# Two buffers for the halves of a slice, and another order of loads, in a fused attention and gMLP block

## The chip, the cores and the metric

The kernel runs on one core of one Trainium2 chip. The metric is the device time of one execution in microseconds (us); three timed runs of the kernel before gave 698.01, 703.25 and 704.19 us, so the median is 703.25 us.

## The reference

The input is one sequence of S = 2048 rows of D = 1024 bf16 numbers. First comes a pre-normalised attention with a sliding, dilated window (8 keys, every second row back), then a pre-normalised gated MLP that mixes the rows with a 2048 x 2048 matrix `w_sp`:

```
h  = x + attention(layernorm(x), wqkv) @ wo
z  = gelu(layernorm(h) @ w_in)            # [S, 3584], halves z1 and z2 of 1792 columns
z2 = layernorm(z2)
g  = einsum('ts,bsf->btf', w_sp, z2) + b_sp
out = h + (z1 * g) @ w_out                # w_out: [1792, 1024]
```

## The kernel before, in words

The first part, up to about 429 us of the profiled execution, computes the attention and both halves of z. Its instructions are ordered by a small planner in the kernel itself. z1 (transposed) and z2 are written to memory on the device, `z1_d` and `z2_d`, and read back later. The change does not touch this part, except that the first w_out load is issued near its end.

The second part is written out by hand, instruction by instruction, and so is the order of the DMA queue of SyncE (SP) in it. It runs two passes (`pr` = 0 and 1), each over 1024 rows t of the result. A pass has NQ = 7 groups (`i` = 0 to 6); group n = 7 pr + i takes 256 columns of z2 and forms w_sp @ z2 for them by Strassen's scheme: seven products instead of eight. Each product is eight matmuls of 128x128 by 128x512 (`times`, L1091). In a group the TensorE order is fixed: k1 (straight from the slice, block a11), k4, k3, k2 (from differences and sums of blocks of the slice, the tiles `zs`, made by `z_form` on VectorE one group ahead), then the second halves of k1 (block a12), k4 (block a22) and k3 (`zs` number 4). A slice is 2048 rows by 256 columns, 1 MB, held as [128, 16, 256]: its first half (row tiles 0 to 7) holds a11 and a21, its second half (row tiles 8 to 15) a12 and a22. `load_z2f(n, hf)` loads half hf of slice n; `z_form(n+1, 3)` reads the first half of slice n+1 alone, `z_form(n+1, 1)` both halves.

While a group's products run, ScalarE copies the first parts of k1, k4 and k3 out of PSUM (L1228 to L1232, into `p`), then does two side jobs of the first pass: row sums of |w_sp| (`row_sum`, L908, of rows that ScalarE itself loads as `wn`, L904) and column sums of |w_out| (`wout_sum`, L1135). VectorE makes the four `zs` of the next group (L988) and then the results of this one: L1285, L1290, L1292, the scaling of z1 (`z1_scaled`, L1145 on ScalarE or L1147 on VectorE), L1298 to L1300. GpSimd (POOL) adds in L1244, L1286, L1287 and L1291.

In group 5 of the first pass the scales are derived: `row_scales(1)` (L912 to L918) needs all row sums, `wout_level` (L1151 to L1156) all w_out sums, and both follow, in VectorE's order, everything that VectorE does for group 4. Two small transposes on TensorE (L1238, L1239) take their results. They stand in TensorE's order between k2 and the second part of k1 of group 5.

Four kinds of loads feed the first pass:
- z2 slices, one per group, two groups ahead, on SP's queue (L980);
- z1 pieces, `z1c`, 512 KB per group, one group ahead, on SP's queue (L1104); it waits for VectorE's L1300 of the group before, which frees its buffer;
- the next pass's part of w_sp, transposed on the way in by DMA (`load_raw(2, ...)`, L953, tile `rawa`), in four quarters of 512 KB, on SP's queue, in groups 1 to 4;
- w_out, 3.5 MB, on GpSimd's queue (`load_wout`, L1140), in groups 0 to 4.

The order on SP's queue in a group is: z1 piece n+1, at the group's end both halves of slice n+2, then the transposed quarter.

Of the kernel before, what the change touches and what calls it, by code (L numbers as in the profile page):

```python
# [11 lines left out]
BF16 = mybir.dt.bfloat16  # L12
# [10 lines left out]
P = 128  # L23
NT = S // P
CH = 512
NCH = S // CH
TPC = CH // P
# [19 lines left out]
HK = S // P // 2  # L47
# [85 lines left out]
def kernel(  # L133
# [14 lines left out]
    dma = nc.sync.dma_start  # L148
    dma_w = nc.gpsimd.dma_start
# [38 lines left out]
    def wtile(shape, name, tag):  # L188
        return w16.tile(shape, BF16, name=name, tag=tag)
# [760 lines left out]
    def load_raw(c, lo=0, hi=TPC):  # L950
        if lo == 0:
            raw[c] = wtile([P, NT, CH], "rawa", "wB") if c % 2 == 0 else zpools["z"].tile([P, NT, CH], BF16, name="rawb")
        nc.sync.dma_start_transpose(raw[c][:, :, lo * P:hi * P], wsp_view[c * CH + lo * P:c * CH + hi * P])  # L953
# [19 lines left out]
    z2f, zs = {}, {}  # L973
    z2_view = z2_d[:].rearrange("(k p) f -> p k f", p=P)

    def load_z2f(n, hf):
        if hf == 0:
            z2f[n] = zpools["z"].tile([P, NT, 2 * P], BF16, name="z2f", tag="z2f", bufs=2)
        i = n % (NF // 2)
        dma(z2f[n][:, hf * HK:(hf + 1) * HK, :], z2_view[:, hf * HK:(hf + 1) * HK, 2 * i * P:(2 * i + 2) * P])  # L980

    def z_form(n, m):
        z = z2f[n]
        a11, a21, a12, a22 = z[:, 0:HK, 0:P], z[:, 0:HK, P:2 * P], z[:, HK:NT, 0:P], z[:, HK:NT, P:2 * P]
        t = zs[n, m] = zpools["z"].tile([P, HK, P], FP16, name="zs", tag="zs", bufs=5)
        x, y, op = {3: (a11, a21, ALU.subtract), 1: (a21, a22, ALU.add), 2: (zs[n, 1][:] if m == 2 else None, a11, ALU.subtract),
                    4: (a12, zs[n, 2][:] if m == 4 else None, ALU.subtract)}[m]
        V.tensor_tensor(t[:], x, y, op=op)  # L988
# [37 lines left out]
    zpools = {}  # L1026
# [60 lines left out]
    NQ = NF // 2  # L1087

    def times(dst, wts, mov, first, lo=0, hi=HK, last=HK):
        for k in range(lo, hi):  # L1090
            T.matmul(dst, wts(k), mov(k), start=(first and k == 0), stop=(k == last - 1), skip_group_check=not first)  # L1091

    def slab(t):
        return lambda k: t[:, k, :]

    def f32(name):
        return p2.tile([P, CH], FP32, name=name, tag=name)
# [3 lines left out]
    def load_z1c(n):  # L1101
        pr, i = divmod(n, NQ)
        z1cs[n] = p2.tile([P, 2, 2 * CH], BF16, name="z1c", tag="z1c", bufs=2)
        dma(z1cs[n][:], z1_d[2 * i:2 * i + 2, :, 2 * pr * CH:(2 * pr + 2) * CH].rearrange("f p s -> p f s"))  # L1104
# [2 lines left out]
        hrs[t] = p2.tile([P, D], BF16, name="hr", tag="hr", bufs=4)  # L1107
        dma(hrs[t][:], h_d[t * P:(t + 1) * P, :])

    WLOAD = ((0, 4), (4, 8), (8, 10), (10, 12), (12, 14))  # L1110
    WSUM = {1: (0, 1, 2, 3), 2: (4, 5, 6, 7), 3: (8, 9, 10), 4: (11, 12, 13)}
    Z1ACT = (0, 5, 6) + tuple(range(NQ, 2 * NQ))

    small = p2.tile([P, 64], FP32, name="small", tag="small", bufs=1)
# [20 lines left out]
        A.activation(zg[:, NF - 1, :], wout_tile(f), ACTF.Abs, accum_out=l1n[:, f:f + 1])  # L1135

    def load_wout(i):
        lo, hi = WLOAD[i]
        dst = wout_a[:, lo:hi, :] if hi <= 8 else wout_b[:, lo - 8:hi - 8, :]
        dma_w(dst, wout_view[:, lo:hi, :])  # L1140

    def z1_scaled(n):
        z1c, s_ = z1cs[n], sf[:, n % NQ:n % NQ + 1]
# [62 lines left out]
    for pr in range(NCH // 2):  # L1206
# [4 lines left out]
        bt2 = bB[:, (2 * pr + 1) * CH:(2 * pr + 2) * CH]  # L1211
        for i in range(NQ):
            n = pr * NQ + i
            z = z2f[n]
            a11, a12, a22 = z[:, 0:HK, 0:P], z[:, HK:NT, 0:P], z[:, HK:NT, P:2 * P]
            p1, p7, p5, u = f32("p1"), f32("p7"), f32("p5"), f32("u2")
            if n == 0:
                load_z1c(0)
            if n + 1 < 2 * NQ:
                load_z1c(n + 1)  # L1220
            if i == 0:
                zg = p2.tile([P, NF, 2 * CH], FP16, name="zg", tag="zg", bufs=1)
            if n < len(WLOAD):
                load_wout(n)
            z1c = z1cs[n][:].bitcast(FP16)
            k1, k4, k3, k2 = bank_a(), bank(), bank(), bank()
            times(k1[:], slab(a11), slab(b11), True)
            A.copy(p1[:], k1[:])  # L1228
            times(k4[:], slab(zs[n, 3]), slab(t3), True)
            A.copy(p7[:], k4[:])  # L1230
            times(k3[:], slab(zs[n, 1]), slab(t1_), True)
            A.copy(p5[:], k3[:])  # L1232
            times(k2[:], slab(zs[n, 2]), slab(t2_), True)
            if pr == 0 and i == 5:
                row_scales(1)
                wout_level()
                turned = bank(BF16)
                T.transpose(turned[0:TPP, 0:P], rsc16[:, TPP:NT], ident[:])  # L1238
                T.transpose(turned[0:1, P:2 * P], kb[:, 0:1], ident[:])  # L1239
                A.copy(rscT[0:TPP, :], turned[0:TPP, 0:P])  # L1240
                A.dma_start(rs_d[TPP:NT, :], rscT[0:TPP, :])
            times(k1[:], slab(a12), slab(b21), False)
            times(k4[:], slab(a22), slab(t4_), False)
            nc.gpsimd.tensor_tensor(p7[:], p7[:], p5[:], op=ALU.add)  # L1244
            if pr == 0:
                if 1 <= i <= 4:
                    for t in (TPP + 2 * i - 2, TPP + 2 * i - 1):
                        row_sum(t, 0)
                        row_sum(t, 1)
                if i <= 3:  # L1250
                    load_wn2(TPP + 2 * i)
                for f in WSUM.get(i, ()):
                    wout_sum(f)
                if i == 6:
                    for fp in range(1, 5):
                        wout_scaled(fp)
            if i + 1 < NQ:
                for m in (3, 1, 2, 4):
                    z_form(n + 1, m)
                if n == 0:  # L1260
                    V.memset(ones[:], 1.0)
                    feature_scales()
            elif pr == 1:
                for m in (3, 1, 2, 4):
                    s_form(TPC, m, 0, NQ - 1)
            else:
                for fp in range(5, NQ):
                    wout_scaled(fp)
                scale_raw(2, 0)
                scale_raw(2, HK)  # L1270
            if pr == 0 and i == 5:
                wout_turned(turned[0:1, P:2 * P])
                spread = bank()
                T.matmul(spread[:, 0:2], ones[:], kb[0:1, 2:4], start=True, stop=True)
            times(k3[:], slab(zs[n, 4]), slab(b22), False)
            if n + 2 < 2 * NQ:
                for hf in range(2):
                    load_z2f(n + 2, hf)
            if pr == 0 and 1 <= i <= TPC:
                load_raw(2, i - 1, i)  # L1280
            elif n == 5:
                rows_in(1)
            if n in Z1ACT:
                z1_scaled(n)
            V.tensor_tensor(u[:], k2[:], p1[:], op=ALU.add)  # L1285
            nc.gpsimd.tensor_tensor(p1[:], u[:], bt1, op=ALU.add)  # L1286
            nc.gpsimd.tensor_tensor(u[:], u[:], bt2, op=ALU.add)  # L1287
            z11, z12 = zg[:, 2 * i, 0:CH], zg[:, 2 * i, CH:2 * CH]
            z21, z22 = zg[:, 2 * i + 1, 0:CH], zg[:, 2 * i + 1, CH:2 * CH]
            V.tensor_tensor(z11, k1[:], bt1, op=ALU.add)  # L1290
            nc.gpsimd.tensor_tensor(z22, p7[:], u[:], op=ALU.add)  # L1291
            V.tensor_tensor(z21, k4[:], p1[:], op=ALU.add)  # L1292
            if pr == 0 and i == 5:
                wout_spread(spread)
                wout_scaled(0)
            if n not in Z1ACT:
                z1_scaled(n)
            V.tensor_tensor(zg[:, 2 * i + 1, :], zg[:, 2 * i + 1, :], z1c[:, 1, :], op=ALU.mult)  # L1298
# [8 lines left out]
        for q in range(TPC):  # L1307
# [34 lines left out]
            a11, a12, a22 = slab(zz[:, 0, :, c1:c1 + P]), slab(zz[:, 1, :, c1:c1 + P]), slab(zz[:, 1, :, c2:c2 + P])  # L1342
# [94 lines left out]
```

## Time and profile before

| | us |
|---|---|
| median of three timed runs | 703.25 |
| the profiled execution, its own time | 708.02 |
| its span, first to last instruction | 706.2 |
| TensorE busy in the span | 686.5 (97%) |
| VectorE busy | 556.8 (79%) |
| ScalarE busy | 342.4 (48%) |
| GpSimd busy | 159.4 (23%) |
| group 0 of the first pass starts | 429.2 |
| group 6 of the first pass starts | 513.0 |

The profile is of one execution; the time outside its span is 708.02 - 706.2 = 1.8 us. "Idle before" an instruction is how long its engine stood still ahead of it, and the arrow names what ended this. SPq, ACTq and POOLq are the engines' own instruction streams where they issue DMAs; the time of such an issue ends when the engine has handed over its last descriptor, not when the data has landed.

### The profile page before, as it was taken

The page shows a single profiled execution, that of the slowest core. Times are in us where ns is not written, and L with a number is a line of the kernel's source. Part 1 is how long each engine was busy: PE and PEld are TensorE (multiplying, and loading weights), DVE is VectorE, ACT ScalarE, POOL GpSimd, SP SyncE. Part 2 cuts the span into 40 slices and gives each one's busy share as a digit, 9 for nine tenths or more (in the row PEclk, how much of TensorE's full clock was granted, in tenths as well). Part 3 has the DMA queues.
Part 4 walks back from the last instruction along what each step waited for, and adds up shares of the span by engine and source line. Part 5 has one row for each costly group of instructions (what it writes and reads, how often), then busy time and mean ns, then how long its engine had stood idle before and what let it go on. Part 6 is the DMA issues. An engine that isn't in the chain of part 4 may idle for free.

```text
span 706.2 us, 8977 instructions
## 1 busy us (share of the span) xinstructions
PE 686.5 (97%) x3374; PEld 354.5 (50%) x3374; DVE 556.8 (79%) x693; ACT 342.4 (48%) x493; POOL 159.4 (23%) x142
## 2 busy tenths in 40 slices
PE   9999999999999999999999999998699999999996
PEld 7766665566645445444444544443244434444443
DVE  6899899999999799997974485662879778665574
ACT  4547652444328876747754643685370322323231
POOL 0100010011010111100301212443340544543443
PEclk9999999999999999999999999999899999999999
DMA  9978597587994588461946996899676115553032
GB/s 322 321 232 246 161 222 244 150 235 216 269 357 124 164 229 231 168 161 34 204 172 172 243 302 210 270 234 232 156 203 184 59 61 151 149 146 92 0 120 89
DMA packets 145275, 133.05 MB, mean 188 GB/s; under 512 B 68752, under 2 KB 117296, under 8 KB 145104
## 3 DMA queue, kind: packets, MB, share of 16 engines
q1 hardware_dynamic: 132720, 88.93, 45.0%
q0 software_dynamic: 7856, 32.97, 17.0%
q10 hardware_dynamic: 4656, 10.59, 4.4%
q8 instruction: 26, 0.43, 0.3%
q14 instruction: 17, 0.14, 0.1%
HBM read 75.25 MB, written 33.10 MB: 153 GB/s over the span
## 4 chain that ended last, share of the span: by engine, by line
PE 77%; issue 8%; DMA 5%; POOL 5%; DVE 4%; SPq 0%; DVEq 0%; ACT 0%; POOLq 0%
PE acc L464 22%; PE acc L796 14%; PE acc L864 14%; PE bank L1091 12%; PE acc L719 8%; PE banka L1091 5%; DMA z2f<-z_d 2%; PE acc L306 2%; DMA hr<-h_d 2%; POOL p L1383 1%; POOL p L1382 1%; DMA rows<-rs_d 1%; DVE hr L1388 1%; PE wps L228 1%; POOL p L1363 1%
## 5 line engine op out<-in xcount | busy, mean ns | idle before, releaser
L864 PE MATMUL acc<-hnT,win 128*128 128x512 bf16 x448 | 98.0, 379 | 0.0
L796 PE MATMUL acc<-win,hnT 128*128 128x512 bf16 (+1 forms) x512 | 98.0, 352 | 0.0
L528 DVE TENSOR_TENSOR prod<-qT,kT 128x4096 bf16<-128x4096 bf16 x32 | 72.7, 2283 | 1.3 <-ACT kT L470 1.3
L796 PEld LDWEIGHTS <-hnT 128*128 128x128 bf16 x512 | 49.9, 98 | 47.4 <-issue 0.7
L1091 PEld LDWEIGHTS <-zs 128*128 128x128 f16 x448 | 43.6, 98 | 54.5 <-DVE zs L988 2.6
L864 PEld LDWEIGHTS <-win 128*128 128x128 bf16 x448 | 43.6, 98 | 52.6 <-issue 0.7
L475 ACT CAST stg<-acc 128x1024 bf16<-128x1024 f32 x36 | 36.4, 1012 | 61.1 <-PE acc L464 52.6
L1091 PE MATMUL banka<-rawa,z2f 128*128 128x512 f16 x224 | 54.2, 386 | 3.2 <-ACT p L1228 2.2
L464 PE MATMUL acc<-xnT,wk 128*128 128x512 bf16 x256 | 56.5, 379 | 0.0
L464 PE MATMUL acc<-xnT,wv 128*128 128x512 bf16 x256 | 56.4, 380 | 0.0
L719 PE MATMUL acc<-wo_sb,av_oT 128*128 128x512 bf16 x256 | 56.1, 379 | 0.0
L1091 PEld LDWEIGHTS <-z2f 128*128 128x128 bf16 x336 | 33.0, 99 | 44.3 <-issue 4.6
L1091 PE MATMUL bank<-rawb,zs 128*128 128x512 f16 x224 | 53.0, 379 | 1.3 <-DVE zs L988 1.3
L1091 PE MATMUL bank<-form,zs 128*128 128x512 f16 x224 | 50.6, 379 | 0.0
L464 PEld LDWEIGHTS <-wk 128*128 128x128 bf16 x256 | 36.5, 143 | 19.0 <-issue 0.8
L464 PEld LDWEIGHTS <-wv 128*128 128x128 bf16 x256 | 36.5, 144 | 18.6 <-issue 0.5
L870 ACT ACTIVATE z1s<-acc 128x1024 bf16<-128x1024 f32 x28 | 28.6, 1022 | 34.6 <-PE acc L864 26.2
L803 ACT ACTIVATE u<-acc 128x1024 bf16<-128x1024 f32 (+1 forms) x32 | 29.3, 915 | 30.9 <-PE acc L796 30.9
L464 PE MATMUL acc<-xnT,wq 128*128 128x512 bf16 x192 | 41.9, 379 | 0.0
L719 PEld LDWEIGHTS <-av_oT 128*128 128x128 bf16 x256 | 25.0, 98 | 30.0
L532 DVE TENSOR_TENSOR prod<-prod 128x2048 bf16<-128x2048 bf16 x32 | 38.8, 1217 | 0.0
L988 DVE TENSOR_TENSOR zs<-z2f 128x1024 f16<-128x1024 bf16 x28 | 20.7, 760 | 22.0 <-DMA z2f<-z_d 18.5
(262 smaller groups left out, 1128.1 us busy)
## 6 DMA issues: line engine op xcount, KB each, us to landing
z2f<-z_d SPq DMA_DIRECT2D x28, 512.0 KB, 6.3
qkv_d<-stg SPq DMA_DIRECT2D x36, 256.0 KB, 4.8
wn<-in_B_w_sp_dram ACTq DMA_DIRECT2D x16, 512.0 KB, 5.2
z1c<-z_d SPq DMA_DIRECT2D x14, 512.0 KB, 4.1
z_d<-z1s SPq DMA_DIRECT2D x21, 256.0 KB, 2.4
z_d<-u SPq DMA_DIRECT2D x12, 448.0 KB, 2.5
av_y<-av_z POOLq DMA_DIRECT2D x4, 1024.0 KB, 9.8
av_oT<-av_zz POOLq DMA_DIRECT2D x4, 1024.0 KB, 15.0
```

The source lines that it names most:

```text
L306: T.matmul(dst.rearrange("p (a b) -> p a b", b=P), wqs[:, kt, dl, :], xnT[0][:, lo:hi, kt, :], start=start, stop=stop)
L464: T.matmul(G[key][:, j, :].rearrange("p (a b) -> p a b", a=TPC), wv[:, kt, dl, :], xnT[c][:, :, kt, :], start=(kt == 0), stop=(kt == KT - 1))
L475: A.copy(stg[:], G[key][:])
L528: V.tensor_tensor(st["prod"][:], qT[:], kT[:, :, o:o + CH], op=ALU.mult)
L532: V.tensor_tensor(dst, p_[:, 0:4, :], p_[:, 4:8, :], op=ALU.add)
L719: T.matmul(st["acc", il][:, nh, :], oTs[c][:, dl, il * P:(il + 1) * P], wo_sb[:, dl, nh * CH:(nh + 1) * CH], start=(dl == 0), stop=(dl == ...
L796: T.matmul(accf[:, n0:n1], hnTs[c][:, il, kt, :], wins[hf][:, kt, n0:n1], start=(kt == 0), stop=(kt == KT - 1))
L803: A.activation(st["u", il][:, hf * 1024:hf * 1024 + wd], G["accz", c, il, hf][:].rearrange("p a b -> p (a b)")[:, 0:wd], ACTF.Gelu_apprx_t ...
L864: T.matmul(G["accy", c, fp][:, j, :].rearrange("p (a b) -> p a b", a=TPC), wt[:, kt, f0 * P:(f0 + 1) * P], hnTs[c][:, :, kt, :], start=(kt ...
L870: A.activation(z1s[:], G["accy", c, fp][:], ACTF.Gelu_apprx_tanh, accum_out=zsum[:, c, fp:fp + 1])
L988: V.tensor_tensor(t[:], x, y, op=op)
L1091: T.matmul(dst, wts(k), mov(k), start=(first and k == 0), stop=(k == last - 1), skip_group_check=not first)
```

## The change

The slice's two halves become two tiles of [128, 8, 256], `z20` and `z21`, each with two buffers (together as large as before). On SP's queue the load of the first half of slice n+2 is issued right after k1's first product of group n; then comes the transposed quarter, now in groups 2 to 5, then the z1 piece; the second half of slice n+2 stays at the group's end. w_out is loaded in groups 0 (1.5 MB in two loads), 1 (1 MB in two loads) and 4 (1 MB in one load), instead of 1, 1, 0.5, 0.5 and 0.5 MB in groups 0 to 4. The w_out sum of row tile 10 moves from group 3 to group 4.

```diff
     def load_z2f(n, hf):
-        if hf == 0:
-            z2f[n] = zpools["z"].tile([P, NT, 2 * P], BF16, name="z2f", tag="z2f", bufs=2)
+        t = zpools["z"].tile([P, HK, 2 * P], BF16, name="z2%d" % hf, tag="z2%d" % hf, bufs=2)
+        z2f.setdefault(n, []).append(t)
         i = n % (NF // 2)
-        dma(z2f[n][:, hf * HK:(hf + 1) * HK, :], z2_view[:, hf * HK:(hf + 1) * HK, 2 * i * P:(2 * i + 2) * P])
+        dma(t[:], z2_view[:, hf * HK:(hf + 1) * HK, 2 * i * P:(2 * i + 2) * P])
...
-    WLOAD = ((0, 4), (4, 8), (8, 10), (10, 12), (12, 14))
-    WSUM = {1: (0, 1, 2, 3), 2: (4, 5, 6, 7), 3: (8, 9, 10), 4: (11, 12, 13)}
+    WLOAD = {0: ((0, 4), (4, 6)), 1: ((6, 8), (8, 10)), 4: ((10, 14),)}
+    WSUM = {1: (0, 1, 2, 3), 2: (4, 5, 6, 7), 3: (8, 9), 4: (10, 11, 12, 13)}
...
     def load_wout(i):
-        lo, hi = WLOAD[i]
-        dst = wout_a[:, lo:hi, :] if hi <= 8 else wout_b[:, lo - 8:hi - 8, :]
-        dma_w(dst, wout_view[:, lo:hi, :])
+        for lo, hi in WLOAD.get(i, ()):
+            dst = wout_a[:, lo:hi, :] if hi <= 8 else wout_b[:, lo - 8:hi - 8, :]
+            dma_w(dst, wout_view[:, lo:hi, :])
...
-            z = z2f[n]
-            a11, a12, a22 = z[:, 0:HK, 0:P], z[:, HK:NT, 0:P], z[:, HK:NT, P:2 * P]
+            za, zb = z2f[n]
+            a11, a12, a22 = za[:, :, 0:P], zb[:, :, 0:P], zb[:, :, P:2 * P]
...
-            if n + 1 < 2 * NQ:
-                load_z1c(n + 1)
...
-            if n < len(WLOAD):
-                load_wout(n)
+            load_wout(n)
...
             times(k1[:], slab(a11), slab(b11), True)
             A.copy(p1[:], k1[:])
+            if n + 2 < 2 * NQ:
+                load_z2f(n + 2, 0)
+            if pr == 0 and 2 <= i < 2 + TPC:
+                load_raw(2, i - 2, i - 1)
+            if n + 1 < 2 * NQ:
+                load_z1c(n + 1)
...
             times(k3[:], slab(zs[n, 4]), slab(b22), False)
             if n + 2 < 2 * NQ:
-                for hf in range(2):
-                    load_z2f(n + 2, hf)
-            if pr == 0 and 1 <= i <= TPC:
-                load_raw(2, i - 1, i)
-            elif n == 5:
+                load_z2f(n + 2, 1)
+            if n == 5:
                 rows_in(1)
```

More of the change, by code (lines that the diff above doesn't have):

```diff
@@ L976, in load_z2f @@
     def load_z2f(n, hf):
-        if hf == 0:
-            z2f[n] = zpools["z"].tile([P, NT, 2 * P], BF16, name="z2f", tag="z2f", bufs=2)
+        t = zpools["z"].tile([P, HK, 2 * P], BF16, name="z2%d" % hf, tag="z2%d" % hf, bufs=2)
+        z2f.setdefault(n, []).append(t)
         i = n % (NF // 2)
-        dma(z2f[n][:, hf * HK:(hf + 1) * HK, :], z2_view[:, hf * HK:(hf + 1) * HK, 2 * i * P:(2 * i + 2) * P])
+        dma(t[:], z2_view[:, hf * HK:(hf + 1) * HK, 2 * i * P:(2 * i + 2) * P])
     def z_form(n, m):
-        z = z2f[n]
-        a11, a21, a12, a22 = z[:, 0:HK, 0:P], z[:, 0:HK, P:2 * P], z[:, HK:NT, 0:P], z[:, HK:NT, P:2 * P]
+        halves = [(t[:, :, 0:P], t[:, :, P:2 * P]) for t in z2f[n]]
+        a11, a21 = halves[0]
+        a12, a22 = halves[1] if len(halves) > 1 else (None, None)
         t = zs[n, m] = zpools["z"].tile([P, HK, P], FP16, name="zs", tag="zs", bufs=5)
@@ L1213 @@
             n = pr * NQ + i
-            z = z2f[n]
-            a11, a12, a22 = z[:, 0:HK, 0:P], z[:, HK:NT, 0:P], z[:, HK:NT, P:2 * P]
+            za, zb = z2f[n]
+            a11, a12, a22 = za[:, :, 0:P], zb[:, :, 0:P], zb[:, :, P:2 * P]
             p1, p7, p5, u = f32("p1"), f32("p7"), f32("p5"), f32("u2")
```

## The prediction

> **What bounds the kernel now.** The page's first part gives TensorE 686.5 of 706.2 us, so time is to be had only where TensorE stands still. The slices of the second part show where: TensorE's row is 9 everywhere but in slices 28 and 29 (and at the very end). I therefore read the waits from 425 to 660 us (the second part, without its last stretch); columns are who waited, for whom, us in total, times, longest.
>
> ```profile
> POOL p L1286 <- DVE u L1285: 55.4, 14, 8.9
> ...
> DVE zs L988 <- DMA z2f<-z_d: 18.5, 8, 9.4
> ...
> PE bank L1238 <- DVE rsc L918: 6.1, 1, 6.1
> ...
> ACT zg L1135 <- DMA wout_b<-in_B_w_out_dram: 5.0, 1, 5.0
> ...
> PE banka L1091 <- ACT p L1228: 2.2, 2, 1.3
> ...
> PE bank L1091 <- DVE wout_b L1188: 1.4, 1, 1.4
> ...
> PE banka L1091 <- DMA z2f<-z_d: 1.0, 1, 1.0
> ```
>
> The long waits of POOL are harmless (POOL is 23% busy). What counts are the four PE lines and the two DMA lines that feed them. The timeline of 450 to 532 us shows how they hang together (start, length, instruction, idle before it):
>
> ```profile
> 469.13 0.72 POOL L1140 DMA_DIRECT2D wout_b<-in_B_w_out_dram  x1
> ...
> 476.02 3.37 SPq L980 DMA_DIRECT2D z2f<-z_d  x2
> ...
> 479.44 13.81 SPq L953 DMA_TRANSPOSE rawa<-in_B_w_sp_dram  x1
> ...
> 483.87 1.06 ACT L1135 ACTIVATE zg<-wout_b 128x1024 f16<-128x1024 bf16 x1 [5.05 <-DMA wout_b<-in_B_w_out_dram]
> ...
> 485.54 1.89 PE L1091 MATMUL banka<-rawa,z2f 128*128 128x512 f16 x8 [0.92 <-ACT p L1228]
> ...
> 491.84 0.69 DVE L988 TENSOR_TENSOR zs<-z2f 128x1024 f16<-128x1024 bf16 x1 [9.35 <-DMA z2f<-z_d]
> ...
> 491.86 1.90 PE L1091 MATMUL banka<-rawa,z2f 128*128 128x512 f16 x8 [0.98 <-DMA z2f<-z_d]
> ...
> 505.00 0.27 PE L1238 MATMUL bank<-ident,rsc 128*8 128x128 bf16 x1 [6.06 <-DVE rsc L918]
> ```
>
> Slice 5, issued at 476.02 at the end of group 3, lands its first half only at 491.84, 15.8 us later, where the DMA part gives a median of 6.3. VectorE sits 9.35 us on it, does group 4's results late, and so the scales, for which TensorE waits at 505.00. The w_out load of 469.13 lands at 483.87 and holds up ScalarE's copies. The stage's windows show why both are late (columns: us, busy by engine, clock, DMA share, GB/s):
>
> ```profile
> 474.00:477.00 3.00, 3.00 (x16) 1.37 (x14) 2.69 (x5) 2.10 (x5) 0.62 (x1) 1.00 1.10 61
> 477.00:480.00 3.00, 3.00 (x16) 1.35 (x15) 1.75 (x2) 1.79 (x4) 2.84 (x3) 1.00 1.60 93
> 480.00:483.00 3.00, 3.00 (x16) 1.35 (x15) 1.99 (x3) 0.00 (x0) 1.10 (x2) 1.00 0.54 142
> ...
> 504.00:507.00 3.00, 1.19 (x4) 0.44 (x5) 2.72 (x14) 0.25 (x1) 0.00 (x0) 0.50 0.57 169
> ```
>
> For 9 us the DMA engines moved 61 to 142 GB/s though at first fully busy; in the trace's packets, a transposed quarter (256-byte packets) and a w_out load (4096-byte) are there together: the quarter's packets go from 18 to about 340 ns, w_out's from 170 to about 1400 ns. A quarter alone needs 1.8 us (three in a row from 403.3 to 408.8).
>
> **What TensorE loses.** A product takes 1.727 us (441.29 to 443.02 and so on), a group seven, 12.09. Against this pace: group 4's second k1 product starts at 485.54 instead of 477.55 + 4 x 1.727 = 484.46, 1.08 late. Group 5 starts at 491.86 instead of 488.99 + 1.73 = 490.72: 1.14. In group 5 products stop from 495.33 + 3.45 = 498.78 to 506.28, of which the two transposes need 0.4: 7.10. The product after the pause, 506.28 to 509.33, takes 3.05, as the clock column says 0.50: 1.32. Sum 10.64 us. At the passes' border VectorE is late with `wout_b` (L1188): 1.4.
>
> The Trainium skill (TensorE: Matmul & The Clock Gate, Part 1) says that an idle window of about 3.4 us halves the array's clock, and about as much work restores it. The trace agrees (0.50 after 6 us without work). By it a pause kept under that length would also save the 1.32.
>
> **The change, step by step.** T is a group's start.
>
> *First half early.* It waits for k1 of group n (T + 1.73), not for the end of the sixth product (T + 10.36; 451.85 in group 1, which started at 441.29). No instruction is added: the same 28 loads of 512 KB. Unobstructed, a half shows its first packet 1.0 us after issue and takes 2.0 to 2.3 (439.76: 440.78 to 443.04). So it lands near T + 5 instead of next T + 5 to 9. k1 of group n+2 can't wait for it any more: 1.14 saved.
>
> *Transposed quarter.* It now follows one half on its ring, not two, and w_out has left groups 2 and 3; from T + 2.5, done by T + 8. SP is held meanwhile: its issue ran 6.4 to 13.8 us before, until the slice ahead of it had drained; ahead lies now half of that, 3 to 6 us. Behind it wait the z1 piece (T + 6 to 8; needed by VectorE at next T + 11.5, as group 1's L1147 at 452.53 shows) and the second half of slice n+2, which is not free before T + 10.4 anyway. The cover is 3 us for the latter and some 13 for the former; a collapse like that at 474 would eat the first. The second half then lands after 3 to 6 us, next T + 2 to 5; group 1's `zs` 1 ran at T + 4.4. So the 9.35 falls to between 0 and 3. Worth by itself: VectorE ends group 4 at next T + 3 (group 1: 456.25 = T + 15.0) instead of T + 11.9 (503.77).
>
> *w_out.* Group 0 gets 0.5 MB more at 415, among the first slices: at some 300 GB/s 1.7 us, bounded by 0 and 3.0 (128 packets took 3.0 there). It delays `zs` 1 of group 0, ready at 426.79 and needed at 432.66: hidden; without this cover it would cost up to 3. Group 3's sums have their data: 1.08 saved. Group 4's 1 MB is new risk. POOL issues it after group 3's L1291, T + 0.4 to 2.8 (453.52, 480.38); first packets come 1.9 to 4.4 us later; 1 MB took 4.7 (444.39 to 449.12). Done at T + 7 to 12. ScalarE is through the row sums at T + 10.3 (group 1: 451.42), four sums at 1.18 end at T + 15 to 17, and `wout_level` 1.1 later (504.86 to 505.98). The transposes are due at T + 12.09 + 6.9 = T + 19. Slack 1 to 3 us; so group 5's 7.10 and 1.32 go. I leave 1.0 us as a remainder, between 0 and the 5 of the first rival, nearer the loads that met nothing.
>
> *Passes' border.* The scaled rows come some 1 us earlier for the same reason, so of the 1.4 between 0 and 1.4 go; I take 0.8. The second pass (586 to 655 us) shows no TensorE wait on loads: nothing.
>
> **Sum.** 10.64 - 1.0 + 0.8 = 10.4 us from the profiled execution's own 708.02: 697.6. That execution stands 4.8 above the median. If these 4.8 are stalls that the timed runs lacked, the timed result is near 697.6; if they are a constant, 703.25 - 10.4 = 692.9. The three runs spread over 6.2 us, so some of the stall varies; I take the middle, **695.0 us**, own range 691 to 699.
>
> **The rivals.**
> 1. *The w_out load of group 4 collapses with that group's quarter.* Both start near T + 5. In the collapse the 0.5 MB of 473.49 ended at 483.19, 9.7 us instead of 3.0: 6.7 more. Landing T + 17, sums T + 21.5, level T + 22.6: TensorE waits 3.6 and up to 1.3 for the clock, about 5. Time 695 + 4 = 699. For it: the timing. Against: 474 also followed a backlog of `wn` and two slice halves.
> 2. *The stall isn't in the timed runs.* 698.01 may be a run with little of it; then 701 to 703 stays. Against: the first two runs are 5 us longer.
> 3. *Slower.* The same collision with all 256 w_out packets inside it: 19.4 us from T + 7, landing T + 26.5, sums T + 31.2, level T + 32.3, TensorE waits 13.3 + 1.3; with slice 6 and the z1 piece late behind the quarter, some 3 more at the border. That is 17.6 against 10.6 now: 703.25 + 7 = 710. It decides from a landing at T + 22.5 on (22.5 + 5.8 - 19 + 1.3 = 10.6, what is lost now). For it: twice the bytes in one load. Against: quarters at 490 and 500, without w_out, lost only 1 to 2 us.
>
> The Trainium skill (DMA: Bandwidth & Descriptors, Issuing engines are not separate DMA queues) speaks against the change: all queues share the same 16 DMA engines and interleave. The trace agrees that the streams delay each other at 474; so spreading the loads helps only where a group had more than it could move, and rivals 1 and 3 are what that sharing would do in group 4.
>
> **How the numbers follow.** Forecast 0.62, rival 1 0.17, rival 2 0.06, rival 3 0.15. A change of about 1%, 7 us, is what a measurement of this kernel can tell from none; the limits are 696.2 and 710.3. Of the forecast 0.57 lies below 696.2, 0.05 above; rival 1 gives 0.01 to faster and 0.16 to same, rival 2 0.06 to same; rival 3, with nothing but its middle at the limit, 0.13 to slower and 0.02 to same. Faster 0.58, same 0.29, slower 0.13. The range runs from 689 (a constant offset and no remainder, and 2 below for run to run) to 707, leaving most of rival 3 out.
>
> **What would show it.** Right: VectorE's wait on slice 5 falls from 9.35 to under 3; no ScalarE wait on `wout_b` before L1228; L1238 waits under 1.5; group 6 starts 83 - 10 = 73 us after group 0; no clock of 0.50 near 505. Wrong: `wout_b` of group 4 lands after T + 14, 256-byte packets at 340 ns in it, or SP's transposed issue still lasting over 8 us with z1 pieces late at L1147.

## The result and the profile after

The changed kernel takes 696.99 us (median of 14 runs, 696.65 to 697.57). The kernel before took 701.89 in the same comparison (14 runs, 697.80 to 710.51). The ratio is 0.9929, its 95% interval 0.9905 to 0.9953: 0.7% faster, less than the 1% that the prediction set as its limit, but not nothing. The ratios, here and below, leave out the runs more than 1.5% above the fastest of their kernel, and so differ somewhat from the ratio of the medians. As telling as the medians is the spread: 0.9 us after, 12.7 before. The fastest runs before lie within 1 us of the median after.

The profiled execution after has an own time of 697.15 us and a span of 695.4; before they were 708.02 and 706.2. On the profile the gain is therefore 10.9 us. First the page after, TensorE's busy slices and the granted clock:

```profile
span 695.4 us, 8974 instructions
...
PE   8999999999999999999999999999999999999996
...
PEclk9999999999999999999999999999999999999999
```

The hole in slices 28 and 29 is gone. The waits after, again from 425 to 660 us:

```profile
DVE zs L989 <- DMA z<-z_d: 5.1, 4, 2.1
...
DVE zg L1299 <- ACT z1c L1146: 2.5, 1, 2.5
...
PE bank L1092 <- DVE zs L989: 1.4, 2, 0.9
PE bank L1092 <- DVE wout_b L1189: 1.3, 1, 1.3
PE banka L1092 <- ACT p L1226: 1.3, 1, 1.3
```

TensorE's waits for the scales (6.1) and for the slice (1.0) are no longer there, nor is ScalarE's for `wout_b` (5.0). VectorE's waits on slices fell from 18.5 to 5.1. The wait at the passes' border stayed (1.4 before, 1.3 now). The timeline after, at the place of the one shown of before; group 4 starts at 477.31, group 5 at 489.39, group 6 at 502.00:

```profile
475.77 3.81 SPq L980 DMA_DIRECT2D z<-z_d  x2
...
477.31 1.89 PE L1092 MATMUL banka<-rawa,z 128*128 128x512 f16 x8
...
477.45 0.91 POOL L1141 DMA_DIRECT2D wout_b<-in_B_w_out_dram  x1
...
479.64 6.90 SPq L953 DMA_TRANSPOSE rawa<-in_B_w_sp_dram  x1
...
481.75 0.69 DVE L989 TENSOR_TENSOR zs<-z,z 128x1024 f16<-128x1024 bf16 x1 [0.97 <-DMA z<-z_d]
...
490.87 1.06 ACT L1136 ACTIVATE zg<-wout_b 128x1024 f16<-128x1024 bf16 x1
...
494.25 0.16 DVE L1157 CAST kb<-small 128x1 bf16<-128x1 f32 x1
...
496.39 0.22 PE L1242 MATMUL bank<-ident,rsc 128*8 128x128 bf16 x1
...
502.00 1.89 PE L1092 MATMUL banka<-rawa,z 128*128 128x512 f16 x8
```

VectorE waits 0.97 us on slice 5 instead of 9.35, the last w_out sum ends at 492.0, the scales' input `kb` is there at 494.4, two us ahead of the transpose at 496.39, which waits for nothing. Group 0 starts at 428.96, so group 6 follows 73.04 us later: six groups of 12.09 and 0.5 for the small matmuls. In this stretch TensorE loses nothing. I call what it loses here "the loss" below; it was 10.7 us before. The windows of group 4 show that the loads move again (columns: us, busy by engine, clock, DMA share, GB/s):

```profile
477.00:480.00 3.00, 3.00 (x16) 1.37 (x14) 2.86 (x4) 2.13 (x5) 1.36 (x2) 1.00 1.03 374
480.00:483.00 3.00, 3.00 (x16) 1.35 (x14) 1.78 (x4) 0.90 (x2) 0.00 (x0) 1.00 1.05 358
483.00:486.00 3.00, 3.00 (x16) 1.35 (x15) 1.75 (x3) 3.00 (x6) 1.40 (x2) 1.00 1.41 302
504.00:507.00 3.00, 3.00 (x16) 1.35 (x15) 2.92 (x6) 1.23 (x3) 0.00 (x0) 1.00 0.83 208
```

358 and 302 GB/s where the kernel before had 61 to 142 from 474 to 483, and the clock is 1.00 at 504.

### The profile page after: what moved, and what is told of

It reads as the page before. It is cut to its first block, busy times and chain, and to the rows that moved or that the text cites. A ratio compares the mean times of both kernels' runs of the same rounds, so it can differ in the third digit from the quotient of the medians.

```text
span 695.4 us, 8974 instructions
## 1 busy us (share of the span) xinstructions
PE 683.0 (98%) x3357; PEld 353.9 (51%) x3374; DVE 557.1 (80%) x693; ACT 343.0 (49%) x493; POOL 158.4 (23%) x142
## 4 chain that ended last, share of the span: by engine, by line
PE 79%; issue 9%; DVE 5%; POOL 5%; DMA 2%; SPq 0%; DVEq 0%; ACT 0%; POOLq 0%
PE acc L464 22%; PE acc L864 14%; PE acc L796 14%; PE bank L1092 13%; PE acc L719 8%; PE banka L1092 5%; PE acc L306 2%; DMA hr<-h_d 2%; POOL p L1384 1%; POOL p L1383 1%; DVE hr L1389 1%; POOL p L1364 1%; DVE zs L989 1%; POOL zg L1292 1%; POOL p L1382 1%
## 5 line engine op out<-in xcount | busy, mean ns | idle before, releaser
L1092 PE MATMUL banka<-rawa,z 128*128 128x512 f16 x224 | 52.9, 379 | 1.3 <-ACT p L1226 1.3
L1092 PEld LDWEIGHTS <-z 128*128 128x128 bf16 x336 | 32.8, 98 | 41.0 <-issue 1.6
L464 PEld LDWEIGHTS <-wq 128*128 128x128 bf16 x192 | 27.5, 143 | 13.9
```

The lines of the kernel that those rows point to most:

```text
L464: T.matmul(G[key][:, j, :].rearrange("p (a b) -> p a b", a=TPC), wv[:, kt, dl, :], xnT[c][:, :, kt, :], start=(kt == 0), stop=(kt == KT - 1))
```

## The experiments

The questions were which of the three parts (early half, place of the quarters, places of w_out) brings the gain, and what the collapse of the loads is. The kernel before ran again beside them; over all comparisons it has 108 runs from 697.35 to 710.97, 23 of them under 698.5 and 41 over 704.8. The loss given with each kernel is that of its one profiled execution. Added to the 697.15 us of the profiled execution after, it gives the own time of every profiled execution within 0.6 us, with one exception (the quarters one group later, 701.00 us), where more is lost at the passes' border.

### One part alone

**w_out's new places alone**, on the kernel before.

```diff
-    WLOAD = ((0, 4), (4, 8), (8, 10), (10, 12), (12, 14))
-    WSUM = {1: (0, 1, 2, 3), 2: (4, 5, 6, 7), 3: (8, 9, 10), 4: (11, 12, 13)}
+    WLOAD = {0: ((0, 4), (4, 6)), 1: ((6, 8), (8, 10)), 4: ((10, 14),)}
+    WSUM = {1: (0, 1, 2, 3), 2: (4, 5, 6, 7), 3: (8, 9), 4: (10, 11, 12, 13)}
...
```

> The kernel before with the new places of the w_out loads and sums alone. Theory A (a transposed quarter and a w_out load of GpSimd's queue that meet on the DMA engines stop each other, and this is the loss): groups 2 and 3 now hold a quarter and no w_out load, so slice 5 lands in time, VectorE's longest wait on a slice is under 4 us, the transposes of group 5 wait under 1.5 us, and the time is 697 to 699 us. Theory B (too many bytes wait at a group's end behind both slice halves, and only the early first half cures this): VectorE still waits 6 us or more on slice 5, TensorE 4 us or more at the transposes, 700 to 703 us.

Measured: 700.09 (698.70 to 704.51, 10 runs), ratio 0.9979 [0.9942, 1.0016], loss 3.3. The collision is not gone but moved into group 4. In the trace's packets w_out runs from 485.1 to 492.1 and the quarter from 482.8 to 489.6, while the quarters of groups 2 and 3, now without w_out beside them, take 2.4 and 2.3 us. Windows of this kernel, and ScalarE in its timeline:

```profile
486.00:489.00 3.00, 3.00 (x15) 1.37 (x14) 2.23 (x5) 1.49 (x4) 1.38 (x2) 1.00 0.75 89
```

```profile
492.78 1.06 ACT L1135 ACTIVATE zg<-wout_b 128x1024 f16<-128x1024 bf16 x1 [5.28 <-DMA wout_b<-in_B_w_out_dram]
```

89 GB/s, and ScalarE waits 5.28 us for w_out: this is rival 1 of the prediction, in a kernel without the other two parts. Its interval includes 1: these runs don't tell it from no change.

**Quarters one group later alone**, still at the group's end.

```diff
-            if pr == 0 and 1 <= i <= TPC:
-                load_raw(2, i - 1, i)
-            elif n == 5:
+            if pr == 0 and 2 <= i < 2 + TPC:
+                load_raw(2, i - 2, i - 1)
+            if n == 5:
```

> The kernel before with the transposed quarters one group later (groups 2 to 5, still at the group's end, behind both slice halves), nothing else. Theory A: the quarter issued at the end of group 2 meets the w_out load of group 3 as before, and those of group 4's w_out too; nothing is cured: 700 to 704 us with the runs spread over some 5 us or more as in the kernel before. Theory B: group 1's bytes fall, group 5's rise: 699 to 703 us.

Measured: 701.52 (701.00 to 702.98), ratio 0.9984 [0.9950, 1.0018]. The loss is only 0.8, but the last quarter is late at the passes' border, where TensorE waits 1.5 and 1.8 us for `wout_a` and `wout_b` (and its clock falls to 0.50 for 3.4 us) and VectorE 2.9 for a load. Group 4 again has both streams together: w_out from 484.6 to 492.1, the quarter from 482.8 to 490.8. 701.52 lies in the ranges of both theories; theory A's spread of some 5 us or more isn't there, it is 2.0.

**Halves in buffers of their own alone**: tiles and first half as in the change, quarters and w_out as before.

```diff
-        if hf == 0:
-            z2f[n] = zpools["z"].tile([P, NT, 2 * P], BF16, name="z2f", tag="z2f", bufs=2)
+        t = zpools["z"].tile([P, HK, 2 * P], BF16, name="z2%d" % hf, tag="z2%d" % hf, bufs=2)
...
             A.copy(p1[:], k1[:])
+            if n + 2 < 2 * NQ:
+                load_z2f(n + 2, 0)
...
-                for hf in range(2):
-                    load_z2f(n + 2, hf)
+                load_z2f(n + 2, 1)
```

> The kernel before with the two buffers per half and the early first half alone; z1 piece, quarters and w_out loads at their old places. Theory A: a quarter still meets the w_out load of group 3; the first half of slice 5 is safe, the second half, the w_out load and ScalarE's sums are not: ScalarE still waits 2 us or more on w_out, TensorE loses 3 to 8 us in groups 4 and 5, 699 to 702 us. Theory B: the early half takes half of the bytes off the group's end: 697 to 698.5 us.

Measured: 701.33 (697.42 to 703.79), ratio 0.9978 [0.9939, 1.0018], loss 2.6. Here the collision is in group 2: w_out from 458.3 to 465.8, the quarter from 456.9 to 465.4, at 139 and 137 GB/s in its windows from 459 to 465. So no part alone makes a difference that these runs can tell from none.

### All but one part

**The change without its w_out part**: after.py with the old lists, in groups 0 to 4.

```diff
-    WLOAD = {0: ((0, 4), (4, 6)), 1: ((6, 8), (8, 10)), 4: ((10, 14),)}
-    WSUM = {1: (0, 1, 2, 3), 2: (4, 5, 6, 7), 3: (8, 9), 4: (10, 11, 12, 13)}
+    WLOAD = {0: ((0, 4),), 1: ((4, 8),), 2: ((8, 10),), 3: ((10, 12),), 4: ((12, 14),)}
+    WSUM = {1: (0, 1, 2, 3), 2: (4, 5, 6, 7), 3: (8, 9, 10), 4: (11, 12, 13)}
```

> The changed kernel with the w_out loads and sums back in their old places (1, 1, 0.5, 0.5, 0.5 MB in groups 0 to 4), so that only this part is undone. Theory A: the quarters, now at T + 5 of groups 2 to 4, run just when the w_out loads of those groups do (first packets at T + 2 to 7): a collision, 256-byte packets of 340 ns, ScalarE waiting on w_out, 699 to 703 us and a spread of several us. Theory B: the order of SP's queue is what matters: 697 to 698 us, as the changed kernel.

Measured: 697.27 (nine of ten runs from 696.89 to 697.86, one at 701.39), ratio 0.9926 [0.9888, 0.9964], loss 0.3. Nearly all of the gain is there without the part that I had given w_out; the theory with 699 to 703 fell. In group 3 w_out (469.2 to 473.0) and the quarter (472.4 to 478.5) hardly overlap. The quarter still needs 6.1 us there, with only 0.01 MB of w_out beside it, so it is stretched beside other loads too; here nothing waits for it.

**The change with the quarters back at the groups' ends**, in groups 1 to 4, all else kept.

```diff
-            if pr == 0 and 2 <= i < 2 + TPC:
-                load_raw(2, i - 2, i - 1)
...
-            if n == 5:
+            if pr == 0 and 1 <= i <= TPC:
+                load_raw(2, i - 1, i)
+            elif n == 5:
```

> The changed kernel with the transposed quarters back at the end of groups 1 to 4, behind the second half of a slice; halves, z1 order and w_out places as changed. Theory A: the quarter issued at the end of group 3 has its packets at some T + 4 to 7 of group 4, where the 1 MB of w_out runs: they meet, w_out lands late for its four sums, ScalarE waits 3 us or more and TensorE loses 2 to 5 us: 698.5 to 702 us. Theory B: the early first half is still there, so 697 to 698.5 us.

Measured: 700.65 (696.71 to 704.83), ratio 0.9984 [0.9946, 1.0022], loss 5.7: the gain is gone (its interval touches that of the change only at its end), and the spread is back. Its windows in group 4, and then its timeline:

```profile
480.00:483.00 3.00, 3.00 (x15) 1.36 (x14) 1.78 (x3) 1.24 (x3) 0.00 (x0) 1.00 1.14 211
483.00:486.00 3.00, 3.00 (x15) 1.37 (x14) 1.62 (x4) 3.00 (x7) 1.75 (x2) 1.00 1.45 153
486.00:489.00 3.00, 3.00 (x15) 1.37 (x14) 1.90 (x3) 1.10 (x3) 2.84 (x3) 1.00 1.08 107
```

```profile
494.40 1.06 ACT L1136 ACTIVATE zg<-wout_b 128x1024 f16<-128x1024 bf16 x1 [7.31 <-DMA wout_b<-in_B_w_out_dram]
...
499.13 0.17 DVE L1152 TENSOR_TENSOR small<-small 128x7 f32<-128x7 f32 x1 [6.10 <-ACT zg L1136]
...
500.36 0.26 PE L1241 MATMUL bank<-ident,kb 128*1 128x128 bf16 x1 [4.08 <-issue]
```

w_out (482.4 to 493.6) meets the quarter (480.5 to 490.8), ScalarE waits 7.31 us for it, VectorE 6.10 for ScalarE, and TensorE 4.08 in turn ("issue" here stands where `kb` is due). This is the chain of rival 1.

**w_out's last load in group 3 instead of 4**: of the change, one key.

```diff
-    WLOAD = {0: ((0, 4), (4, 6)), 1: ((6, 8), (8, 10)), 4: ((10, 14),)}
+    WLOAD = {0: ((0, 4), (4, 6)), 1: ((6, 8), (8, 10)), 3: ((10, 14),)}
```

> The changed kernel with the last w_out load (1 MB) issued in group 3 instead of group 4: 12 us earlier, so it can't be late for its sums, but its first packets come at T + 2 to 5 and it lasts 5 us, while the group's transposed quarter runs at T + 5 to 8.5. Theory A: the two meet and stretch each other to some 8 us or more, 256-byte packets well over 100 ns on average; behind them the z1 piece and the second half of slice 5 are late; 698 to 702 us and a spread of 2 us or more. Theory B (only the order on SP's queue matters) and rival C: an earlier load costs nothing, 696.5 to 697.5 us, spread under 1 us.

Measured: 697.59 (697.28 to 698.81), ratio 0.9948 [0.9914, 0.9983], loss 1.6. It lies some 0.6 us above the change, not at the 698 to 702 that one theory wanted, and just above the 696.5 to 697.5 of the other. w_out runs from 468.6 to 473.8, the first half of slice 5 beside it from 471.0 to 475.1, and only then the quarter, 473.0 to 478.4. The half has its packets beside w_out's and holds the quarter back: a shield, which the change has in group 4 too.

**Place alone**: before, with the quarters right behind k1 of groups 2 to 5 and the z1 piece behind them, but no early half in front.

```diff
-            if n + 1 < 2 * NQ:
-                load_z1c(n + 1)
...
             A.copy(p1[:], k1[:])
+            if pr == 0 and 2 <= i < 2 + TPC:
+                load_raw(2, i - 2, i - 1)
+            if n + 1 < 2 * NQ:
+                load_z1c(n + 1)
...
-            if pr == 0 and 1 <= i <= TPC:
-                load_raw(2, i - 1, i)
-            elif n == 5:
+            if n == 5:
```

> The kernel before with the transposed quarters right behind k1 of groups 2 to 5 and the z1 piece behind them, as in the changed kernel, but without the early first half (both halves still at the group's end, one tile) and with w_out at its old places. Theory A with the shield (in the changed kernel the quarter waits on its ring behind half a slice, which itself shares with w_out, so w_out is through first): without that half the quarter starts at T + 3.5 to 4.5, into the w_out loads of groups 2 to 4 (first packets T + 2 to 5): they meet, 698.5 to 703 us and a spread of 3 us or more. Theory B2 (the quarter's place before the group's end is enough): 697 to 697.6 us and a spread under 1.5 us.

Measured: 701.55 (697.76 to 710.23), ratio 1.0012 [0.9962, 1.0062], loss 4.7. Without the half the quarter (470.8 to 475.6) goes straight into w_out (473.4 to 478.3); windows of this kernel:

```profile
471.00:474.00 3.00, 3.00 (x15) 1.37 (x14) 2.04 (x2) 3.00 (x7) 1.27 (x1) 1.00 1.28 142
```

So the place needs the half ahead of it (701.55 without it, 697.27 with it, both with w_out's old places), and the half needs the place (701.33 without it, against the same 697.27).

### The border

Both pieces of `wform(B12, ...)`, which makes `wout_b` for TensorE's wait at the passes' border, ahead of the next product's form instead of one before and one after.

```diff
-                wform(B12, B22, B12, (0,))
+                wform(B12, B22, B12)
...
-                wform(B12, B22, B12, (1,))
```

> The changed kernel with one more edit: at the border of the two passes VectorE makes both pieces of B12 before T4, instead of T4 between them. TensorE's wait on wout_b (L1189 of the changed kernel, 1.3 us and 1.46 with its start) goes, since T4 is needed 5 us later: 695.3 to 695.8 us against 697.0 of the changed kernel. If VectorE's sum of work there is the limit, the wait only moves to T4's product and the time stays at 696.7 to 697.2.

Measured: 696.76 (696.42 to 697.26, 12 runs), ratio 0.9933 [0.9896, 0.9970]; 0.23 us under the change, which is too little to call: the runs of the two overlap and come from separate comparisons. The wait of 1.30 us is gone, but the next one has grown. The same matmul, first in the change and then in this kernel:

```profile
561.66 1.90 PE L1092 MATMUL bank<-rawb,zs 128*128 128x512 f16 x8 [0.41 <-DVE zs L989]
```

```profile
561.47 1.90 PE L1092 MATMUL bank<-rawb,zs 128*128 128x512 f16 x8 [1.66 <-DVE zs L989]
```

0.41 became 1.66: what TensorE waits for there is VectorE's sum of work, not its order, and the time is inside the 696.7 to 697.2 that was expected for this case.

### What the collision is

**The loads alone.** A kernel that computes nothing of the reference (its output is a copy of x): 2 MB of w_sp transposed (as much as four quarters, tile `quarter`), 2 MB of w_out, 1 MB in 512-byte pieces, alone and in pairs, each pair beginning when the one before has landed. In the code, `turn` loads the transposed part on SP's queue, `big` w_out and `small` the 512-byte pieces, on the queue of the engine named.

```diff
+        lambda: turn(),
+        lambda: big(nc.gpsimd),
+        lambda: big(nc.scalar),
+        lambda: small(nc.scalar),
+        lambda: (big(nc.gpsimd), turn()),
+        lambda: (big(nc.scalar), turn()),
+        lambda: (small(nc.scalar), turn()),
...
```

> Loads alone, with none of the computation (the result is a copy of x): a 2 MB transposed part of w_sp on SP's queue, 2 MB of w_out in 4096-byte packets on GpSimd's or on ScalarE's queue, and 1 MB in 512-byte packets on ScalarE's queue, first each by itself, then the transposed part together with each of the others, twice. Theory A (a transposed quarter and a w_out load stop each other on the DMA engines): by itself the transposed part takes 7 to 8 us and w_out 9 to 10; together on GpSimd's queue they take far more than the sum, 25 us or more, with 256-byte packets of some 300 ns and 4096-byte ones of over 1000 ns. If it is the GpSimd queue, ScalarE's queue gives no more than the sum, some 17 us; if it is the packets' size, both queues give the same. Rival C (plain sharing of bandwidth): every pair takes the sum of its two times, 16 to 18 us with w_out, within 2.

Measured, as VectorE's waits for the later of the pair, in its timeline (the transposed load with GpSimd's w_out, with ScalarE's, with the 512-byte pieces; then the first two again):

```profile
83.46 0.69 DVE L46 TENSOR_TENSOR junk<-slices,quarter 128x1024 bf16<-128x1024 bf16 x1 [23.68 <-DMA quarter<-in_B_w_sp_dram]
...
100.54 0.69 DVE L46 TENSOR_TENSOR junk<-slices,quarter 128x1024 bf16<-128x1024 bf16 x1 [15.92 <-DMA quarter<-in_B_w_sp_dram]
...
115.79 0.69 DVE L46 TENSOR_TENSOR junk<-slices,quarter 128x1024 bf16<-128x1024 bf16 x1 [14.10 <-DMA quarter<-in_B_w_sp_dram]
...
139.82 0.69 DVE L46 TENSOR_TENSOR junk<-slices,quarter 128x1024 bf16<-128x1024 bf16 x1 [22.88 <-DMA quarter<-in_B_w_sp_dram]
...
157.06 0.69 DVE L46 TENSOR_TENSOR junk<-slices,quarter 128x1024 bf16<-128x1024 bf16 x1 [16.09 <-DMA quarter<-in_B_w_sp_dram]
```

From issue to landing w_out alone took 9.6 us on GpSimd's queue and 8.6 on ScalarE's, and the transposed load alone 9.7 (at the end of the next kernel; in this one it stood behind the copy of x in SP's queue and took 22.9). One after the other that is 19.3 and 18.3. The pair on GpSimd's queue takes 23.7 and 22.9, so about 4 more than the sum; that on ScalarE's takes 15.9 and 16.1, about 2 less. In the trace's packets, 602 and 557 of the 8192 256-byte ones of the slow pairs took over 100 ns, 14 and 17 in the pairs on ScalarE's queue. Theory A's 25 us or more was somewhat too high. So such a loss needs nothing but the two loads. GpSimd's load went in 4096-byte packets and ScalarE's in 2048-byte ones, so this left open whether the queue or the packet decides.

**Large packets from another array.** The same with whole rows of w_sp, 4096-byte packets on either queue (again no part of the reference is computed).

```diff
+        eng.dma_start(wout[:].rearrange("p (a b) n -> p a (b n)", b=2), B_w_sp.rearrange("(a p) s -> p a s", p=P)[:, 4:8, :])
...
+        lambda: (rows(nc.gpsimd), turn()),
+        lambda: (rows(nc.scalar), turn()),
```

> Loads alone again, none of the computation (the result is a copy of x): 2 MB of whole w_sp rows, 4096 contiguous bytes each, on GpSimd's queue and on ScalarE's, by themselves and each twice beside the 2 MB transposed part on SP's queue. In the run before, w_out went in 4096-byte packets on GpSimd's queue and in 2048-byte ones on ScalarE's, so queue and packet size were mixed. Theory A1 (it is GpSimd's queue): GpSimd's pair takes 22 to 24 us, ScalarE's some 16, as before. Theory A2 (it is the 4096-byte packet): both pairs take 22 to 24 us. Rival C (plain sharing): both 16 to 17.

Measured: 17.4 and 15.5 us with GpSimd's queue, 15.5 and 15.1 with ScalarE's. The rows without a transposed load took 10.6 and 12.5, but the copy of x still ran beside them. Even against the times of as many bytes of w_out by themselves (19.3 and 18.3 with the 9.7 of the transposed load) every pair is quicker than the sum. The first pairs of the two queues in the timeline:

```profile
54.06 0.69 DVE L52 TENSOR_TENSOR junk<-slices,quarter 128x1024 bf16<-128x1024 bf16 x1 [17.44 <-DMA quarter<-in_B_w_sp_dram]
70.74 0.69 DVE L52 TENSOR_TENSOR junk<-slices,quarter 128x1024 bf16<-128x1024 bf16 x1 [15.52 <-DMA quarter<-in_B_w_sp_dram]
```

Theories A1 and A2 wanted 22 to 24 us, so neither the queue nor the packet's size alone makes the loss.

**w_out on ScalarE's queue** in the kernel before.

```diff
-        dma_w(dst, wout_view[:, lo:hi, :])
+        A.dma_start(dst, wout_view[:, lo:hi, :])
```

> The kernel before with only the issuing engine of the w_out loads changed, from GpSimd to ScalarE, at the same places of the program; order on SP's queue, groups and buffers as before. The loads still run beside the transposed quarters. Theory A1 (GpSimd's queue and the transposed quarter stop each other): no 256-byte packets over 100 ns on average, no wait of 6 us at the transposes, 697 to 699 us and a spread under 2.5 us. Theories B and C (order on SP's queue, or bytes): the same bytes at the same time, 700 to 705 us with the old spread of 6 us or more.

Measured: 703.14 (699.75 to 707.24), ratio 1.0015 [0.9963, 1.0067], loss 9.3. The quarter takes 470.4 to 480.9 beside w_out's packets, though these now have 2048 bytes and come from another engine. SP and TensorE in its timelines:

```profile
477.00 14.28 SPq L953 DMA_TRANSPOSE rawa<-in_B_w_sp_dram  x1
```

```profile
502.95 0.27 PE L1238 MATMUL bank<-ident,rsc 128*8 128x128 bf16 x1 [5.54 <-DVE rsc L918]
```

The theory that GpSimd's queue is to blame fell. The Trainium skill (DMA: Bandwidth & Descriptors, Issuing engines are not separate DMA queues) says that all issuing engines feed the same 16 DMA engines. This run agrees: another issuer bought nothing.

**Plain quarters**: before, the four quarters loaded without transposing, from the same rows, on the same queue, in the same places and 256-byte pieces. This leaves out the transposition of that part of w_sp.

```diff
-        nc.sync.dma_start_transpose(raw[c][:, :, lo * P:hi * P], wsp_view[c * CH + lo * P:c * CH + hi * P])
+        if c == 2:
+            dma(raw[c][:, :, lo * P:hi * P], wsp_view[c * CH + lo * P:c * CH + hi * P])
+        else:
+            nc.sync.dma_start_transpose(raw[c][:, :, lo * P:hi * P], wsp_view[c * CH + lo * P:c * CH + hi * P])
```

> The kernel before with the four quarters of the next pass loaded by plain DMAs instead of transposing ones: same queue, same place in the order, same 512 KB, same pieces of 256 bytes, same buffer; the part left out is the transposition of that half of w_sp. Theory A (it takes a transposing DMA beside a w_out load): no stretch of either, slice 5 in time, TensorE's wait at the transposes of group 5 under 1.5 us, 697 to 698.5 us with a spread under 2 us. Theories B and C (bytes, small pieces and the order at a group's end): the stretch stays, 700 to 704 us with a spread of 6 us or more.

Measured: 697.83 (ten of eleven runs from 697.14 to 697.87, one at 702.14), ratio 0.9962 [0.9926, 0.9998], loss 0.3. Its windows, over the time in which the kernel before moved 61 to 142 GB/s:

```profile
474.00:477.00 3.00, 3.00 (x15) 1.36 (x14) 2.23 (x5) 2.10 (x5) 1.41 (x2) 1.00 0.87 274
477.00:480.00 3.00, 3.00 (x15) 1.36 (x14) 1.84 (x3) 2.94 (x7) 2.92 (x3) 1.00 1.03 353
480.00:483.00 3.00, 3.00 (x15) 1.36 (x14) 2.25 (x4) 1.13 (x3) 0.24 (x1) 1.00 1.12 320
```

The issue of the quarter at group 3's end took 13.81 us before; here it is:

```profile
476.96 2.23 SPq L954 DMA_DIRECT2D rawa<-in_B_w_sp_dram  x1
```

The same bytes in the same pieces: 256-byte packets at 22 to 24 ns on average, w_out's at 202 ns. In group 3 the plain quarter (470.7 to 473.4) is nearly through when w_out (473.0 to 475.0) begins. In group 4 the two do run together, the quarter from 482.9 to 487.0 and w_out from 484.2 to 487.6. In the kernel with the quarters one group later, where both start within 0.5 us of these times and the quarter is transposed, the two need 8.1 and 7.5 us instead of 4.1 and 3.4. So in these executions the collapse takes a transposing load. Taking it away leaves a kernel that is within 1 us of the changed one, and as steady but for one run.

**Together.** The loss before is a transposed quarter meeting a w_out load. Meeting is not enough: in group 2 of the kernel before the quarter (459.0 to 463.2) also runs beside w_out (457.9 to 461.5), and both are through in 4.2 and 3.5 us, against 10.9 and 9.7 in group 3. In group 3 264 of the quarter's 2048 packets took over 100 ns and 31 of w_out's 128 over 300. The collision is also only the first part of slice 5's delay: its first packet comes 7.5 us after the issue, and its packets then run from 483.5 to 492.9 beside w_out, and beside `wn` and a z1 piece that had been held up too.

How long the two hold each other up differs between executions, which fits the spread. The kernels whose profile shows the collision spread over 5.8 to 13.6 us (2.0 where the quarters come later), those without it over 0.7 to 1.5, but for the one outlier each in two of them. The granted clock, which is on record for 94 runs of the kernel before, adds to this: all 55 runs at 0.996 or less took 701.18 us or more, all 39 at 0.998 or more took 700.67 or less. In the profiled executions the clock falls inside the second part only after pauses of TensorE, so each long run very likely holds one. That a collision made the pause in each of them is argued, since only one execution was profiled.

The change puts the first half of a slice ahead of the quarter; the half shares the DMA engines with w_out, and the quarter comes after both. It needs the place (without it: 700.65), and the place needs the half (without it, and with w_out's old places: 701.55); it hardly needs the places of w_out (without them: 697.27). Alone, those places moved the collision to group 4. That they do no harm there in the change because of the half is argued from the packets: no kernel had both new places without the half.

## Why the prediction held, and where not

The time forecast, 695.0 with an own range of 691 to 699, holds the 696.99 measured. The chances leaned the wrong way: "faster by over 1%" had 0.58, and it is 0.7%.

- **The sum on the profiled execution: right.** 10.4 us were predicted from 708.02, to 697.6; it came to 697.15. The four terms of TensorE's loss (1.08, 1.14, 7.10, 1.32) are all gone. The remainder of 1.0 was nothing, and of the 0.8 at the border 0.1 came. That the sum is right within 0.5 us is in part luck: these two errors nearly cancel.
- **From the profiled execution to the timed runs: the mis-sized step.** I had 697.6 if the 4.8 us above the median "are stalls that the timed runs lacked" and 692.9 if they are a constant, and took the middle. The measured 696.99 is the first. The middle, 695.0, had no reading behind it, and that the range held is owed to its width. Before's runs, from 697.35 to 710.97, look like executions with anything from none of the stall to all of it, and after's profiled execution lies 0.16 from its median: there was no constant to carry over. Rival 2, "the stall isn't in the timed runs", is half of this: it is in some of them, so that before's median moved between 699.6 and 704.9 from comparison to comparison.
- **First half early and second half late: right.** The second half of slice 5 has its packets from 477.84 to 481.18, 0.5 to 3.9 us into group 4 (predicted done at 2 to 5), and VectorE's 9.35 fell to 0.97 (predicted 0 to 3).
- **The packets at 474: read too strongly.** "From 18 to about 340 ns" and "from 170 to about 1400 ns" hold for some of the stretched packets, not for the streams. Half of the quarter's packets still took 18 ns; of those over 100 ns most took 155 to 350, and of the 31 of w_out over 300 ns the median is 1460.
- **The quarter: right in group 3, late in group 4.** In group 3 it was done at T + 8.6, as predicted (T + 8). In group 4 it ran from T + 7.8 to T + 10.8. The half ahead of it had packets only from 483.13 to 486.25, partly beside w_out's 480.7 to 484.7, and the quarter's first packet came 0.5 us after w_out's last. I had counted the half as something that delays the quarter by its own 2 to 3 us. That it keeps the quarter out of w_out's way I had not seen. With the quarter at the group's end instead, rival 1's chain did come (700.65), so rivals 1 and 3 failed here for a reason that the prediction didn't have. SP's issue took 6.90 us there (predicted 3 to 6).
- **w_out in group 4: right in its times, wrong in its worth.** It was done at T + 7.4 (T + 7 to 12), the sums at T + 14.7 (T + 15 to 17, so just ahead of it). But I gave the 1.08 of group 4 and part of the rest to w_out's leaving groups 2 and 3. The change without this part has a loss of 0.3 and 697.27.
- **The passes' border: wrong in size.** Of 1.4 us I took 0.8 as saved; 0.1 was. The rows did come earlier (VectorE takes them 4.9 instead of 5.6 us after group 6's start), but VectorE then waits 2.5 us for ScalarE's scaled z1:

```profile
517.53 0.69 DVE L1299 TENSOR_TENSOR zg<-zg,z1c 128x1024 f16<-128x1024 f16 x1 [2.51 <-ACT z1c L1146]
...
530.01 0.81 PE L1092 MATMUL bank<-wout_b,sf 128*128 128x512 f16 x3 [1.30 <-DVE wout_b L1189]
```

- **The clock: right.** Without the pause no window near 505 shows less than 1.00.

What stays open: why a quarter beside w_out collapses in one group and not in another of the same execution; why w_sp's rows beside a transposed load cost less than the sum while w_out's cost 4 us more; why w_out from ScalarE's queue shares fairly when alone and collides inside the kernel; and the single outliers of the change without its w_out part (701.39, at a clock of 0.998, so without a pause that cost the clock) and of the plain quarters (702.14, at 0.996, so with one).

## What to carry to other kernels

When the runs of a kernel spread over more than the gain that is argued about, price the change on the profiled execution's own time and ask which runs hold that stall at all; the profile's distance from the median is no constant to carry over. When a transposing load and a bulk load run at the same time, look at the packets of both: with nothing else running, w_out on GpSimd's queue beside it cost some 4 us more than one after the other, rows of w_sp cost nothing. Where they do hold each other up, an ordinary load that is due anyway, put ahead of the transposing one on its own queue, can keep the two apart. Before crediting a part of a change, take that part out: here the one with the most lines of argument, w_out's places, was worth some 0.3 us, which these runs can't tell from nothing.

## What the runs showed that I had not expected

- A transposed load of 2 MB and 2 MB of w_out can need 23.7 us together, with nothing else running, against 19.3 one after the other. Inside the kernel the DMA engines fell to 61 to 142 GB/s where a transposed quarter met w_out in group 3; with plain quarters they kept 274 to 353 in the same windows.
- The issue of a transposed quarter holds SP for 3.4 to 14.3 us, longest right after a collision (13.8 and 14.3); the plain quarters' issues took 1.2 to 2.2.
- How short a pause costs the clock. In the kernel with w_out's places alone TensorE paused 2.06 us and the next product took 1.90; in the one with the halves alone it had 0.22 us of work within 2.5, and again the next took 1.90; in the one with the place alone it had 0.22 us of work within 3.2 and the next product took 3.36, at a clock of 0.54; after 4.08 us in the kernel with the quarters back it took 3.30. So here the clock was kept after 2.5 us and lost after 3.2; whether the border is the same at every moment no run shows. The trace's record of the clock has it low for 3.41 us in these last two kernels and for 6.83 in the kernel before. The Trainium skill (TensorE: Matmul & The Clock Gate, Part 1) gives an idle window of about 3.4 us; the trace agrees within some tenths, as the clock was lost at 3.2.
